# Transposed tiles copied out of PSUM by VectorE while the first pass leads by over 30 steps, with new per-stretch constants

## Chip, cores and metric

One core of one Trainium2 chip runs the whole kernel in one launch. The metric is the device time of that launch in microseconds (us). Engines: TensorE (PE, with PEld for its weight loads), VectorE (DVE), ScalarE (ACT), GpSimd (POOL), and SyncE (SP), which issues the DMAs.

## What is computed

Two layers over 2048 tokens of 512 channels, 32 heads of 16 channels, an FFN of 1792. Both layers use the same weights.

```python
def _A_ref(x, wqkv, wo):                       # attention, Dh = 16
    qkv = (x @ wqkv).reshape(B, S, 3, H, Dh).transpose(2, 0, 3, 1, 4)
    q, k, v = qkv[0], qkv[1], qkv[2]
    scores = jnp.einsum("bhqd,bhkd->bhqk", q, k) * (Dh ** -0.5)
    p = _softmax(scores, axis=-1)
    o = jnp.einsum("bhqk,bhkd->bhqd", p, v)
    return o.transpose(0, 2, 1, 3).reshape(B, S, D) @ wo
def _B_ref(x, w_gate, w_up, w_down):
    return (_gelu(x @ w_gate) * (x @ w_up)) @ w_down
x = x + _A_ref(_layernorm(x), A_wqkv, A_wo)    # layer 0
x = x + _B_ref(_layernorm(x), B_w_gate, B_w_up, B_w_down)
x = x + _A_ref(_layernorm(x), A_wqkv, A_wo)    # layer 1
x = x + _B_ref(_layernorm(x), B_w_gate, B_w_up, B_w_down)
```

## The kernel before

**Units and the two passes.** Four heads make a group (eight groups). Queries are cut into blocks: four of 512 tokens in layer 0, and 512, 512, 512, 256, 256 in layer 1. A unit is one block of queries and one group of heads. Every unit goes through two passes over the scores.

- The *first pass* finds each query's maximum. `p1_emit` makes score tiles with queries on the partitions and 512 keys in a PSUM bank (matmuls of L1648), and VectorE takes the maximum of one or two such tiles in one instruction (L1663) into `PM`. The maximum is written back into spare rows of `QT`, through `MT` and small DMAs on SP's queue, so that the second pass subtracts it inside its matmul.
- The *second pass* (`p2_emit`, `p2_tile`) makes the scores again with keys on the partitions (L1518), ScalarE takes the exponential of one or two banks (L1494) into slots of `SCR` (called `PT` in the code), and `pv_emit` multiplies them with the values into PSUM bank 7 (L1542); a column of ones gives the sums.
- A *fold* moves first-pass work from VectorE to ScalarE. POOL makes the difference of two key blocks (`KD`, L1279), PE makes its scores (L1467), ScalarE takes the Relu of one or two such tiles into `PT` slots (L1474), and one custom VectorE instruction (L1658) adds this to the other block's tile and takes the maximum of the sum, so that one instruction covers two tiles. The pair is then worth two tiles in the count of steps.

**Steps and the lead.** `pos["p1"]` and `pos["p2"]` count work in pairs of 512-wide tiles; each pass has 2048 steps. The lead is `pos["p1"] - pos["p2"]`. The second pass of a unit can start only when the first pass of that unit is done, so the lead can't fall below about one unit (32 steps for 512 queries).

**The order.** All instructions are put into the queues by a planner that runs when the kernel is built. It keeps a clock for each engine and for each tile, and at each turn chooses what PE gets next: first-pass matmuls, second-pass matmuls, a fold, a value product, a piece of a projection or FFN product ("chains", with due times counted in first-pass steps), or a filler matmul (`warm_emit`, L1687). Within an engine the order is that of the planner; between engines there are semaphores. The planner's constants are read every 16 first-pass steps from a row of `PLAN` (129 rows of 21 values), in this order:

```python
SPC, SPLIT, S1C, S2C, OV, LIM, NT, P2B, LAG, LAGT, FL, GL, FX, AHD, DUE, DUEM, PIECE, GP, NPV, PB, OVF = PLAN[stretch[0]]
```

S1C and S2C say how long before VectorE or ScalarE runs dry the next score matmuls are put in; LIM, OV and OVF, by how much a chain may hold these up. Above a lead of LAG the second pass gets more PSUM banks and the first pass is held to single ones. `want_fold` folds while the lead is below n/16 + FL, with n the queries of the block (40 for 512 and FL = 8); while a gelu stage is on, below GL; and in the last 360 first-pass steps (from step 1688) below `GLE` = 20. PIECE and GP are the numbers of matmuls in one piece of a chain.

**Copies out of PSUM.** `transpose_tile` (L816) transposes a 128-token tile by four PE transposes into one PSUM bank (bank 3, at times others) and has it copied to SBUF by `evac`, with `fast=True`: to `XNT` (normalized input of the projections and of the FFN) or to `ATTT` (attention output, ahead of the output projection). `proj` (to `SG`) and `vproj` (to `VP`) call `evac` without `fast`. `evac` puts the copy on VectorE (L686) or ScalarE (L688) as `pick` says:

```python
def pick(dve_ok=True):
    if not can_p1[0] and can_p2[0]:
        return "dve"
    if can_p1[0] and not can_p2[0]:
        return "act"
    if not can_p1[0] and not can_p2[0]:
        return "dve" if clk["dve"] <= clk["act"] else "act"
    return "dve" if pos["p1"] - pos["p2"] > LAGT else "act"
```

`can_p1` and `can_p2` say whether a first-pass or second-pass step can be put in now. With both, the copy goes to VectorE only above a lead of LAGT (84 in most rows). `pick` also places the residual sums (`x_add`) and the products of the up projection (L1234, L1240).

**Stages.** In the profile, block ends in layer 0 lie near 363, 664, 965 and 1267 us (output projection, then layernorm and FFN of that block), in layer 1 near 1599, 1897, 2183, 2350 and 2491 us. The FFN's gelu stage (L1221) stops the second pass while it lasts.

Of the kernel before, what the change touches and what calls it, by code (L numbers as in the profile page):

```python
# [310 lines left out]
def _build(nc, x_in, wqkv, wo, wg, wu, wd, out, layer_blocks=((512, 512, 512, 512), (512, 512, 512, 256, 256)),  # L311
# [16 lines left out]
    with es:  # L328
# [355 lines left out]
        def evac(dst, src, r, w, n, fast=False):  # L684
            if pick() == "dve":
                emit("dve", lambda e: e.tensor_copy(dst, src), r=r, w=w, dur=0.065 + n / (1900.0 if fast else 963.0))  # L686
            else:
                emit("act", lambda e: e.activation(dst, src, ACTF.Copy), r=r, w=w, dur=0.055 + n / 1200.0)  # L688
# [1241 lines left out]
```

## Time and profile before

| | us |
|---|---|
| median of 3 runs (2524.16 to 2528.22) | 2525.06 |
| the profiled execution's own time | 2523.95 |
| span of that profile, first to last instruction | 2522.2 |
| copies to XNT and ATTT on ScalarE (L688), 91 | 37.0 + 19.9 busy |
| copies to XNT and ATTT on VectorE (L686), 5 | 1.7 for the four to XNT |
| DVE idle, 60 to 2400 us | 48 |
| ACT idle, 60 to 2400 us | 128 |

How to read the profile's page: "busy" is the time in which an engine worked; the slices give it in tenths over forty equal parts of the span. The chain of waits goes back from the last instruction, at each step to whatever released it. A group's line reads: line of the kernel, engine, operation, output <- input with shapes, count | busy us, mean ns of one | idle time just before, and what ended it. "issue" is time for which the profile shows no cause. Neighbouring instructions of one engine overlap in their listed durations, so the distance from start to start is the time that one more of them takes.

```profile
PE   8999999999999999999999999999999999999999
DVE  7999999999999999999998999999999999999973
ACT  7799999999999999999979899999999999989996
PEclk9999999999999999999999999999999999999999
```

The granted PE clock is full in every slice, and only the first and the last slices of VectorE and ScalarE are visibly empty.

### The profile page before, as it was taken

To read this page: it belongs to the slowest core of one execution; us is meant where nothing else is said; L and a number is where in the kernel's file an instruction comes from. 1 tells how busy PE (TensorE), PEld (TensorE's weight loads), DVE (VectorE), ACT (ScalarE), POOL (GpSimd) and SP (SyncE) were. 2 spreads that over 40 slices of the span, in tenths; PEclk is the share of its full clock that TensorE was granted. 3 is DMA by queue.
4 is the path that set the end of the run, shared out by engine and by line. 5 is a ranking of instruction groups with operands and counts; after the bars stand their busy time and mean duration, and the time that the engine had idled before them with its cause. 6 is when DMAs were issued, how large, how long until landed. Compare 5 with 4: busy or idle time off the path is not lost.

```text
span 2522.2 us, 68091 instructions
## 1 busy us (share of the span) xinstructions
PE 2409.2 (96%) x29682; PEld 1161.1 (46%) x29881; DVE 2403.7 (95%) x3131; ACT 2353.2 (93%) x3267; POOL 683.9 (27%) x1119
## 2 busy tenths in 40 slices
PE   8999999999999999999999999999999999999999
PEld 3444443445434444344434455434453445534556
DVE  7999999999999999999998999999999999999973
ACT  7799999999999999999979899999999999989996
POOL 4111223321332213431133311341113311442300
PEclk9999999999999999999999999999999999999999
DMA  3110000000000000000000000000000000000000
GB/s 102 38 56 6 4 9 2 4 2 2 8 1 4 2 4 6 3 3 14 13 3 4 17 2 2 8 4 10 2 4 6 6 6 3 4 3 14 2 7 6
DMA packets 27419, 25.07 MB, mean 10 GB/s; under 512 B 9456, under 2 KB 26096, under 8 KB 27120
## 3 DMA queue, kind: packets, MB, share of 16 engines
q1 hardware_dynamic: 27120, 20.71, 2.9%
q8 instruction: 234, 3.83, 0.7%
q14 instruction: 65, 0.53, 0.1%
HBM read 9.70 MB, written 2.10 MB: 5 GB/s over the span
## 4 chain that ended last, share of the span: by engine, by line
PE 42%; DVE 32%; ACT 24%; issue 1%; POOL 0%; ACTq 0%
DVE PM L1663 30%; ACT SCR L1494 22%; PE PS L1648 14%; PE PS L671 12%; PE PS L1542 9%; PE PS L1687 4%; PE PS L1518 3%; ACT SCR L1474 1%; DVE SCR L1658 1%; PE PS L816 1%; ACT AO L1114 0%; PE PS L1467 0%; ACT XNT L688 0%; ACT ATTT L688 0%; ACT SG L688 0%
## 5 line engine op out<-in xcount | busy, mean ns | idle before, releaser
L1663 DVE TENSOR_REDUCE PM<-PS 128x1 f32<-128x512 f32 (+1 forms) x2513 | 2216.6, 944 | 52.0 <-PE PS L1518 24.1
L1494 ACT ACTIVATE SCR<-PS 128x1024 bf16<-128x1024 f32 (+1 forms) x2533 | 2008.2, 899 | 59.2 <-PE PS L1518 43.4
L1648 PE MATMUL PS<-KT,QT 32*128 32x512 bf16 x3923 | 1013.1, 384 | 49.4 <-DVE PM L1663 31.9
L1518 PE MATMUL PS<-QT,KT 32*128 32x512 bf16 (+1 forms) x4608 | 924.0, 360 | 7.5 <-ACT SCR L1494 6.3
L1542 PE MATMUL PS<-VP,SCR 128*128 128x51 bf16 (+1 forms) x16384 | 800.8, 187 | 12.3 <-ACT SCR L1494 8.0
L1542 PEld LDWEIGHTS PS<-VP,SCR 128*128 128x128 bf16 x16384 | 568.3, 96 | 486.8 <-issue 424.8
L1648 PEld LDWEIGHTS PS<-KT,QT 32*128 32x128 bf16 x3923 | 242.2, 91 | 547.8 <-DVE PM L1663 324.5
L1687 PE MATMUL PS<-WV,ZER 128*128 128x240 bf16 x2425 | 425.2, 266 | 4.7 <-ACT SCR L1494 4.5
L1096 POOL TENSOR_TENSOR RL<-ACCS,CM 128x16 f32<-128x16 f32 (+1 forms) x63 | 174.5, 2769 | 564.5 <-ACT ACCS L1086 564.3
L1518 PEld LDWEIGHTS PS<-QT,KT 32*128 32x128 bf16 x4608 | 230.2, 91 | 69.3 <-ACT SCR L1494 42.5
L1687 PEld LDWEIGHTS PS<-WV,ZER 128*128 128x128 bf16 x2425 | 185.1, 96 | 63.9 <-issue 48.5
L1242 POOL TENSOR_TENSOR HT<-HT,AO 128x512 bf16<-128x512 bf16 (+1 forms) x107 | 119.5, 1119 | 236.9 <-ACT AO L1240 236.9
L996 POOL TENSOR_TENSOR PM<-PM 128x16 f32<-128x16 f32 (+2 forms) x130 | 30.2, 232 | 379.1 <-DVE PM L1663 373.9
L1279 POOL TENSOR_TENSOR KD<-KT 128x512 bf16<-128x512 bf16 x72 | 82.9, 1152 | 173.9 <-PE PS L1467 166.0
L671 PE MATMUL PS<-XNT,WU 128*128 128x512 bf16 (+1 forms) x447 | 116.3, 353 | 7.3 <-issue 6.2
L671 PE MATMUL PS<-WD,HT 128*128 128x512 bf16 x381 | 115.5, 380 | 7.2 <-issue 5.4
L671 PE MATMUL PS<-XNT,WG 128*128 128x512 bf16 (+1 forms) x488 | 116.3, 357 | 3.6 <-ACT HT L1221 2.1
L1116 POOL TENSOR_TENSOR X<-X,AO 128x512 f32<-128x512 f32 x46 | 58.3, 1266 | 218.8 <-ACT AO L1114 218.8
L1658 DVE CUSTOM_DVE_ANT_0 SCR<-PS,SCR 128x512 bf16<-128x512 f32 x173 | 111.7, 685 | 3.1 <-PE PS L1467 0.6
L1474 ACT ACTIVATE SCR<-PS 128x512 bf16<-128x512 f32 (+1 forms) x121 | 97.1, 802 | 18.7 <-PE PS L1467 18.3
L1221 ACT ACTIVATE HT<-PS 128x512 bf16<-128x512 f32 (+1 forms) x126 | 69.3, 550 | 36.2 <-PE PS L671 33.4
L671 PEld LDWEIGHTS PS<-XNT,WG 128*128 128x128 bf16 x504 | 39.2, 97 | 55.0 <-issue 29.6
(111 smaller groups left out, 991.0 us busy)
## 6 DMA issues: line engine op xcount, KB each, us to landing
KT<-SG SPq DMA_DIRECT2D x64, 64.0 KB
QT<-MT SPq DMA_DIRECT2D x236, 1.0 KB
QT<-SG SPq DMA_DIRECT2D x56, 64.0 KB
out_dram<-AO SPq DMA_DIRECT2D x16, 128.0 KB, 1.7
WG<-in_B_w_gate_dram SPq DMA_DIRECT2D x4, 448.0 KB, 4.8
WU<-in_B_w_up_dram SPq DMA_DIRECT2D x4, 448.0 KB, 4.7
WD<-in_B_w_down_dram SPq DMA_DIRECT2D x4, 384.0 KB, 4.7
QT<-MT SPq DMA_DIRECT2D x68, 0.5 KB
```

Source lines behind the costliest of these rows:

```text
L671: ins = e.matmul(out_ap, lhsT=l, rhs=r_, start=(i == 0), stop=(i == n - 1))
L1096: emit("pool", lambda e: e.tensor_tensor(RL[:, s, 0:4 * nq], lsum, CM1[:, 0:4 * nq], op=ALU.pow), r=[("ACCS", s), ("CM1",)], w=[("RL", s)] ...
L1242: emit("pool", lambda e, ft=ft, o=o: e.tensor_tensor(HT[:, ft, 0:n], HT[:, ft, 0:n], AO[:, o, 0:n], op=ALU.mult), r=[("AO", o), ("HT", ft) ...
L1279: emit("pool", lambda e: e.tensor_tensor(KD[:, s, :], KT[:, g, ka * 512:(ka + 1) * 512], KT[:, g, kb * 512:(kb + 1) * 512], op=ALU.subtrac ...
L1474: emit("act", lambda e: e.activation(PT[:, s0:s0 + cnt, :], PS[:, bk:bk + cnt, :], ACTF.Relu), r=bks, w=[("PT", s0 + d) for d in range(cnt ...
L1494: emit("act", lambda e: e.activation(dst, src, ACTF.Exp, scale=DH ** -0.5), r=[BK[bk + i] for i in range(cnt)], w=[("PT", i) for i in slot ...
L1518: ins = e.matmul(bank(bk)[:, i * n:(i + 1) * n], lhsT=KT[32 * j:32 * j + 32, g, kt * 128:(kt + 1) * 128], rhs=QT[32 * j:32 * j + 32, s, 0: ...
L1542: ins = e.matmul(acc, lhsT=PT[:, slot, i * n + qt * 128:i * n + (qt + 1) * 128], rhs=AP(VP, (kt * H + 4 * g + j) * 17, [[NTT * H * 17, 128 ...
L1648: ins = e.matmul(bank(b), lhsT=QT[32 * j:32 * j + 32, s, qt * 128:(qt + 1) * 128], rhs=KT[32 * j:32 * j + 32, g, kb * 512:(kb + 1) * 512], ...
L1658: emit("dve", lambda e, i=i, b=b, sl=sl: e.tensor_tensor_reduce(PT[:, sl, :], bank(b), PT[:, sl, :], 1.0, -3.0e38, ALU.add, ALU.max, po[:, ...
L1663: emit("dve", lambda e: e.tensor_reduce(po, PS[:, bs[0]:bs[0] + cnt, :], axis=AX.X, op=ALU.max), r=bks, w=[("PM", sm) + h[1:] for h in hs] ...
L1687: return e.matmul(PS[:, b, NACC:512], lhsT=ZER[:, :], rhs=WV[:, 0, 0:512 - NACC], start=(b != 7), stop=(b != 7), skip_group_check=True)
```

## The change

`evac` puts a copy with `fast` (the transposed tiles alone) on VectorE when the lead is above TRL = 30 and at least one of the two passes can go on; where that does not hold, `pick` decides as before. TRD = 0 asks only that the first pass has begun.

```diff
-           ... HNA=3, TNA=3, PB=1, OVF=0.0, ...
+           ... HNA=3, TNA=3, TRD=0, TRL=30, PB=1, OVF=0.0, ...
@@
         def evac(dst, src, r, w, n, fast=False):
-            if pick() == "dve":
+            if fast and pos["p1"] > TRD and pos["p1"] - pos["p2"] > TRL and (can_p1[0] or can_p2[0]) or pick() == "dve":
                 emit("dve", lambda e: e.tensor_copy(dst, src), r=r, w=w, dur=0.065 + n / (1900.0 if fast else 963.0))
```

95 of the 129 rows of PLAN are replaced (row r holds from first-pass step 16 r on). DUE changes in 43 of them, LAG in 41, GL in 40, S2C in 34, S1C in 31, PIECE in 26, FL in 25, LAGT in 11. Some of them:

```diff
@@ rows 4, 6 (steps 64, 96) @@
-    (0.2, 0.1, 0.55, 0.42, 0.3, -0.05, 1, 0, 22, 84, 8, 20, 0.3, 2.0, 0, 6, 1, 2, 9, 1, 0.0),
+    (0.2, 0.1, 0.55, 0.22, 0.3, -0.05, 1, 0, 22, 84, 8, 20, 0.3, 2.0, 0, 6, 4, 2, 9, 1, 0.0),
-    (0.2, 0.1, 0.55, 0.42, 0.3, -0.05, 1, 0, 22, 84, 8, 20, 0.3, 2.0, 0, 6, 1, 2, 9, 1, 0.0),
+    (0.2, 0.1, 0.55, 0.62, 0.3, -0.05, 1, 2, 22, 84, 8, 20, 0.3, 2.0, 0, 6, 2, 2, 9, 1, 0.0),
...
@@ rows 33, 50 (steps 528, 800) @@
-    (0.2, 0.25, 0.45, 0.42, 0.3, 0.05, 2, 1, 126, 84, 3, 60, 0.3, 2.0, -20, 2, 1, 2, 7, 1, 0.2),
+    (0.2, 0.25, 0.45, 0.42, 0.2, 0.05, 2, 1, 126, 84, -7, 60, 0.3, 2.0, -20, -14, 1, 2, 7, 1, 0.2),
-    (0.3, 0.2, 0.45, 0.42, 0.3, -0.05, 1, 1, 62, 84, 8, 40, 0.5, 1.5, 0, 2, 2, 2, 7, 3, 0.0),
+    (0.15, 0.2, 0.45, 0.32, 0.5, -0.05, 1, 1, 70, 84, -2, 80, -0.1, 2.0, 10, -14, 2, 1, 9, 1, 0.0),
...
@@ rows 67, 68 (steps 1072, 1088) @@
-    (0.1, 0.35, 0.15, 0.52, 0.3, -0.15, 1, 1, 70, 84, 8, 20, -0.3, 1.5, 0, 2, 2, 4, 7, 1, 0.0),
-    (0.1, 0.25, 0.45, 0.32, 0.3, -0.05, 1, 1, 70, 84, 13, 60, -0.1, 2.0, 0, 2, 1, 4, 5, 1, 0.0),
+    (0.1, 0.35, 0.0, 0.52, 0.3, -0.15, 1, 1, 86, 84, 8, 20, -0.3, 1.5, 0, 2, 2, 4, 7, 1, 0.0),
+    (0.1, 0.35, 0.0, 0.62, 0.3, -0.15, 1, 1, 86, 84, 8, 20, -0.3, 1.5, 0, 2, 1, 4, 7, 1, 0.0),
...
@@ rows 117, 120 (steps 1872, 1920) @@
-    (0.15, 0.15, 0.65, 0.02, 0.1, -0.05, 3, 0, 38, 84, 53, 80, 0.3, 2.5, -10, 2, 2, 2, 3, 4, 0.1),
+    (0.15, 0.15, 0.65, 0.02, 0.1, -0.05, 3, 0, 62, 84, 33, 80, 0.3, 4.0, 10, 2, 1, 2, 3, 1, 0.0),
-    (0.4, 0.15, 0.65, 0.42, 0.3, -0.05, 3, 0, 5, 84, 8, 60, 0.3, 3.5, -5, 6, 2, 3, 3, 1, -0.05),
+    (0.15, 0.15, 0.65, 0.02, 0.1, -0.05, 3, 0, 62, 84, 33, 80, 0.3, 6.0, 5, 2, 1, 2, 3, 1, 0.0),
```

More of the change, by code (lines that the diff above doesn't have):

```diff
@@ L311, in _build @@
 def _build(nc, x_in, wqkv, wo, wg, wu, wd, out, layer_blocks=((512, 512, 512, 512), (512, 512, 512, 256, 256)),
-           n_ahead=6, n_pre=6, S1C=0.45, S2C=0.42, OV=0.3, PD=80, FDUE=20, LIM=-0.05, NT=1, AHD=2.0, DUEM=2, FDL2=0, OPD=12, URG=0.3, ft_tok=512, n_pt=8, n_qt=8, SPLIT=0.15, SPC=0.1, PVC=47, WARM=0.55, WARML=0.42, NPV=7, BOOST=0.0, LAG=62, LAGT=84, GP=2, SING=0, DUE=0, END=360, LAGE=10, FD=205, FDL=-10, QD=32, KD_=16, VD=20, FL=8, FMAX=6, NKD=2, FLOOK=2, FX=0.3, GF=1, NSPL=3, HSPL=0, TSPL=1, HNA=3, TNA=3, PB=1, OVF=0.0, LNP=0, FNP=1, NSG=3, LNT=12, HV=16, TW=0.95, HF=60, VS=14, SO=1.0, SF=1, SP=0, FAST=1, TG=0, GS=2, P2B=1, PIECE=2, GL=60, GLE=20, HARD=-1e9):
+           n_ahead=6, n_pre=6, S1C=0.45, S2C=0.42, OV=0.3, PD=80, FDUE=20, LIM=-0.05, NT=1, AHD=2.0, DUEM=2, FDL2=0, OPD=12, URG=0.3, ft_tok=512, n_pt=8, n_qt=8, SPLIT=0.15, SPC=0.1, PVC=47, WARM=0.55, WARML=0.42, NPV=7, BOOST=0.0, LAG=62, LAGT=84, GP=2, SING=0, DUE=0, END=360, LAGE=10, FD=205, FDL=-10, QD=32, KD_=16, VD=20, FL=8, FMAX=6, NKD=2, FLOOK=2, FX=0.3, GF=1, NSPL=3, HSPL=0, TSPL=1, HNA=3, TNA=3, TRD=0, TRL=30, PB=1, OVF=0.0, LNP=0, FNP=1, NSG=3, LNT=12, HV=16, TW=0.95, HF=60, VS=14, SO=1.0, SF=1, SP=0, FAST=1, TG=0, GS=2, P2B=1, PIECE=2, GL=60, GLE=20, HARD=-1e9):
     S = x_in.shape[1]
```

162 rows, old and new, of the table PLAN are left out of this document.

## The prediction

> **What bounds the kernel now.** I read the page's head and busy shares first, then the chain of waits, then the groups of instructions by form, then busy time by stage, and last the order of time around single copies.
>
> ```profile
> span 2522.2 us, 68091 instructions
> PE 2409.2 (96%) x29682; PEld 1161.1 (46%) x29881; DVE 2403.7 (95%) x3131; ACT 2353.2 (93%) x3267; POOL 683.9 (27%) x1119
> PE 42%; DVE 32%; ACT 24%; issue 1%; POOL 0%; ACTq 0%
> DVE PM L1663 30%; ACT SCR L1494 22%; PE PS L1648 14%; PE PS L671 12%; PE PS L1542 9%; PE PS L1687 4%; PE PS L1518 3%; ACT SCR L1474 1%; DVE SCR L1658 1%; PE PS L816 1%; ACT AO L1114 0%; PE PS L1467 0%; ACT XNT L688 0%; ACT ATTT L688 0%; ACT SG L688 0%
> ```
>
> Three engines are nearly full. PE's share is the weakest bound of the three: L1687 (425.2 us by form) is filler that the planner puts into gaps. What can't be dropped is VectorE's maximum over the scores (L1663, first pass) and ScalarE's exponential (L1494, second pass): 2216.6 and 2008.2 us. The transposed copies themselves have 0% of the chain, so nothing is gained at their own place; they count as engine time. By stage (busy us: PE, PEld, DVE, ACT, POOL):
>
> ```profile
> 60.00:360.00 300.00, 285.94 (x3677) 143.57 (x3681) 295.62 (x418) 280.10 (x320) 51.08 (x105) 1.00 0.08 23
> 700.00:940.00 240.00, 228.97 (x2915) 109.06 (x2934) 236.16 (x310) 231.57 (x304) 65.73 (x88) 1.00 0.01 3
> 1260.00:1300.00 40.00, 38.23 (x245) 14.10 (x248) 36.50 (x56) 28.53 (x44) 14.58 (x25) 1.00 0.02 5
> 1300.00:1590.00 290.00, 281.34 (x3482) 135.21 (x3500) 276.26 (x351) 268.21 (x344) 72.58 (x98) 1.00 0.02 6
> 2400.00:2522.00 122.00, 115.91 (x1556) 69.70 (x1558) 68.73 (x109) 95.36 (x143) 6.56 (x13) 1.00 0.02 7
> ```
>
> DVE is at 98.5% in the first two rows and idles 3.5 and 13.7 us in the two stages around the change of layer. Over the fifteen such stages that make up 60 to 2400 DVE idles 48 us and ACT 128 (length less busy, added). From 2400 on the first pass runs out (its last reduce starts at 2469.5) and ACT's second pass ends the chain. So DVE is the tighter engine up to 2400, ACT behind it, and neither alone sets the end.
>
> **The change, part one: who copies.** Which tiles move follows from the lead of the first pass at each copy. I counted it in the trace: a 1024-wide reduce is one step, a 512-wide half a step, a custom one (L1658) one step with its folded partner; likewise the exponentials. Both counts end at 2048. At the 91 copies that ACT now makes,
>
> ```profile
> L688 ACT ACTIVATE XNT<-PS 128x512 bf16<-128x512 bf16 x60 | 37.0, 624 | 10.2 <-PE PS L816 9.8
> L688 ACT ACTIVATE ATTT<-PS 128x512 bf16<-128x512 bf16 x31 | 19.9, 643 | 2.2 <-PE PS L816 2.1
> L686 DVE COPY XNT<-PS 128x512 bf16<-128x512 bf16 x4 | 1.7, 419 | 2.4 <-PE PS L816 2.4
> ```
>
> the lead is 0 to 21 for 13 in the head, 0 for three in the tail, 29.5 for two near 2210 us, and 30.5 to 78.5 for the other 73. So 73 move (63 up to 1923 us, ten behind). The floor of the lead is about 40 because the planner folds when it falls below n/16 + FL = 32 + 8; a threshold of 30 lies under it. New rows with FL at -2 or -7 lie at some clusters, but there the lead would still have to fall by ten steps first, and the eight copies of a cluster cost DVE only 2.3 steps; I take 70 to 75.
>
> The profile's durations overlap for neighbours, so the price is the distance from a start to the next start:
>
> ```profile
> 31.50 2.06 ACT L688 ACTIVATE XNT<-PS 128x512 bf16<-128x512 bf16 x4
> 33.40 0.67 ACT L791 ACTIVATE X<-HT 128x512 f32<-128x512 bf16 x1
> 952.15 0.41 DVE L686 COPY XNT<-PS 128x512 bf16<-128x512 bf16 x1
> 952.48 1.21 DVE L1663 TENSOR_REDUCE PM<-PS 128x2 f32<-128x1024 f32 x1
> 953.62 0.69 DVE L763 BATCH_NORM_STATS2 ST<-X 128x6 f32<-128x512 f32 x1
> ```
>
> ACT: (33.40 - 31.50)/4 = 0.475 us a copy, DVE: 952.48 - 952.15 = 0.33. Removed from ACT: 73 x 0.475 = 34.7 us. Added to DVE: 73 x 0.33 = 24.1. Nothing else is issued by a copy: no DMA, no POOL or SP instruction. The wait is the same (for the four transposes of L816) but now DVE's: behind it in that queue stand the next reduces, and for those wait the first-pass matmuls that need their banks (324.5 us of weight-load idle is already put down to L1663). If a copy reaches DVE before PE is done, the loss is of the size that DVE copies show now: 3.2 us over five (2.4 XNT, 0.8 ATTT), 0.64 each, all of it in head and tail. The one DVE copy between 360 and 2400 (952.15) started within its queue's run of work and waited for nothing, so I price this wait at 0, with one such wait for each of ten clusters, 6.4 us, as the other end.
>
> What the time makes of 34.7 off and 24.1 on has three values. If DVE alone binds and nothing is given back: **+24.1**. If ACT alone binds: **-34.7**. Between them lies the exchange that the kernel already has: a folded pair replaces two 1024-wide reduces (2 x 1.14 = 2.28 us, 953.62 - 952.48 each) by two custom ones, and costs one 1024-wide Relu on ACT:
>
> ```profile
> 1277.23 0.69 DVE L1658 CUSTOM_DVE_ANT_0 SCR<-PS,SCR 128x512 bf16<-128x512 f32 x1
> 1277.84 0.69 DVE L1658 CUSTOM_DVE_ANT_0 SCR<-PS,SCR 128x512 bf16<-128x512 f32 x1
> 1278.45 0.69 DVE L1658 CUSTOM_DVE_ANT_0 SCR<-PS,SCR 128x512 bf16<-128x512 f32 x1
> 1267.47 1.03 ACT L1474 ACTIVATE SCR<-PS 128x1024 bf16<-128x1024 f32 x1
> 1268.38 0.62 ACT L688 ACTIVATE ATTT<-PS 128x512 bf16<-128x512 bf16 x1
> ```
>
> 2.28 - 2 x 0.61 = 1.06 us saved on DVE for 0.91 on ACT. For the 63 early copies, DVE +20.8 and ACT -29.9 are level after 50.7/1.97 = 26 pairs: DVE 20.8 - 27.3 = **-6.5**, ACT -29.9 + 23.4 = -6.5. Folds (173 custom instructions now) do occur up to 1942.7 us, and the rule makes them exactly when the lead falls. Behind step 1688 (about 2010 us) the code folds only below a lead of 20; there the ten late copies are worth between +3.3 (DVE) and -4.8 (ACT, which ends the chain); I take 0. Part one: **-6.5**.
>
> The Trainium skill, page "Perfetto Trace Analysis", section "Optimizing Scalar/DVE Operations", speaks against the move: an operation that DVE does quicker may still belong on Scalar when DVE is saturated. The trace agrees with both halves (0.33 against 0.475 us; DVE at 98.5%), and by that rule the value to take would be DVE's +24.1.
>
> **Part two: the constants.** 95 of 129 rows differ. They issue nothing and take nothing away; they move the moment at which instructions are put into the queues (S1C, S2C, LIM), who gets banks (LAG, P2B), when folds are made (FL, GL) and how projections are cut (PIECE, GP). None of this shows as an operation, so it is bounded by idle time. From above: a new order can lose what the worst stage loses now; 1300 to 1590 idles 13.7 us on DVE in 290, 4.7%, against 1.5% in 700 to 940; if a quarter of the span got that way, 2340/4 x 3.2% = +19. From below: if the stages from 1260 to 1590 came down to 1.5% idle, DVE would win 17.2 - 5.0 = 12 us, and from ACT's 19.9 idle us in 60 to 360 some 3 more through folds: -15. The rows at steps 1056 to 1103 (1260 to 1310 us), where the idle time lies, are changed, and those of 1600 to 1700 hardly. Between the ends I take **-3**, nearer to none than to either, since the idle of the saturated stages (1.5%) is what most rows can act on.
>
> **Sum.** -6.5 - 3 = -9.5 against the profiled execution (span 2522.2, run 2523.95), which lies 1.1 below the median of the runs shown, 2525.06. Forecast **2515.5 us**, own range 2508 to 2520.
>
> **Rivals.** (1) *The stages around the change of layer close up*: part two reaches its -15, with part one -6.5: 2503.5. For it: 17.2 us of DVE idle in 330, mostly behind second-pass matmuls (L1518, 11.6 us between 1260 and 1600). Against: it falls where the lead stands at 50 to 80 because the second pass stands for the gelu stage, and the change leaves that stage as it is. (2) *Covered*: the lead falls from 40 to 33, no fold is made in exchange, and the next gelu stage, where the lead rises to 70 or 80 anyway, makes the copies free on both sides: 2525, between 2520 and 2530. For it: after each cluster the lead grows by 20 to 40 steps. Against: DVE has no idle time in which to hide 24 us except 48 in all, spread over 2340. (3) *DVE becomes the bound at the block ends*: at 363, 635, 949, 1599 and 1897 us the lead stands at its floor, each copy delays the reduces behind it, PT slots or the gelu stage keep folds from being made, and ScalarE's second pass, one unit behind, stands for the same time. Price 24.1 less what the last ten and the 16 copies around the layer change (leads of 47 and more) don't cost, 26 x 0.33 = 8.6: +15.5, 2540.5. It decides once fewer than 12 of the 26 pairs are folded (20.8 - 12 x 1.06 - 3 = +5). For it: DVE 98% busy; against: folds are triggered by this very lead.
>
> **How the numbers follow.** A measurement of this kernel can tell about 0.2% (5 us) from no change, so faster means below 2520.0 and slower above 2530.1. Forecast 0.42, rival 1 0.20, rival 2 0.17, rival 3 0.21. Faster: 0.42 + 0.20, less 0.01 for the forecast's upper edge: 0.61; same 0.18; slower 0.21. The predicted time is the forecast's. The range takes in rival 1 with 5 us beyond it, rival 2, and the near edge of rival 3: 2498 to 2532.
>
> **What would show it.** Line L686 should have some 78 XNT and ATTT copies on DVE at about 0.41 us, L688 some 18 on ACT. L1658 should rise from 173 by some 50; busy time of DVE and ACT should both fall by about 6 to 7 us. If L1658 stays and DVE's busy time grows by 20 or more, rival 3 holds; if the lead after the clusters is lower and the span the same, rival 2; if idle time of DVE between 1260 and 1590 halves, rival 1. Wrong would be, above all, copies that wait on DVE for L816 by more than a microsecond a cluster, or a span that changes through stages in which no copy was moved.

## The result, and the profile after

Ten runs of each: 2532.05 us (2531.44 to 2534.34) with the change against 2524.86 (2524.16 to 2528.22) before, a ratio of 1.0028, 95% interval 1.0020 to 1.0036. The kernel became 7 us slower; forecast were 2515.5 us and a gain.

The head of the page after, its chain by engine, and the groups that answer to those of before:

```profile
span 2530.2 us, 68181 instructions
PE 2421.0 (96%) x29691; PEld 1165.8 (46%) x29897; DVE 2416.6 (96%) x3202; ACT 2343.3 (93%) x3252; POOL 683.8 (27%) x1126
PE 44%; DVE 36%; ACT 19%; issue 1%; POOL 0%; ACTq 0%
L1663 DVE TENSOR_REDUCE PM<-PS 128x2 f32<-128x1024 f32 (+1 forms) x2473 | 2196.5, 950 | 47.6 <-PE PS L1518 24.7
L1494 ACT ACTIVATE SCR<-PS 128x1024 bf16<-128x1024 f32 (+1 forms) x2583 | 2014.5, 875 | 72.7 <-PE PS L1518 51.9
L1658 DVE CUSTOM_DVE_ANT_0 SCR<-PS,SCR 128x512 bf16<-128x512 f32 x191 | 123.3, 686 | 4.5 <-PE PS L1648 1.6
L1474 ACT ACTIVATE SCR<-PS 128x512 bf16<-128x512 f32 (+1 forms) x131 | 106.1, 810 | 21.0 <-PE PS L1467 20.6
```

The copies, in the views of the tiles XNT and ATTT (shortest, median and longest ns; first and last start):

```profile
L686 DVE COPY XNT<-PS x46: 377/415/425, 10.3 to 2374.9; 128x512 bf16<-128x512 bf16 x46
L688 ACT ACTIVATE XNT<-PS x18: 591/597/641, 19.5 to 2508.2; 128x512 bf16<-128x512 bf16 x18
L686 DVE COPY ATTT<-PS x31: 382/414/425, 362.5 to 2499.8; 128x512 bf16<-128x512 bf16 x31
L688 ACT ACTIVATE ATTT<-PS x1: 597/597/597, 2499.6 to 2499.6; 128x512 bf16<-128x512 bf16 x1
```

So 77 copies are on VectorE where 5 were: 72 moved (73 by the new rule, and `pick` sends one fewer). L1658 rose from 173 to 191: nine more folded pairs. VectorE is busy 12.9 us longer (2416.6 against 2403.7) and idle 4.9 us less (span less busy: 113.6 against 118.5); the difference is the 8.0 us of the span. ScalarE is busy 9.9 us less and waits more, 51.9 us instead of 43.4 for second-pass matmuls. On this balance alone the case looks like rival 3, VectorE as the bound. The stages shown before, after the change (the last one now ends at 2530):

```profile
60.00:360.00 300.00, 288.86 (x3675) 143.46 (x3678) 294.95 (x430) 282.14 (x319) 52.40 (x108) 1.00 0.08 23
700.00:940.00 240.00, 232.21 (x2909) 110.96 (x2928) 236.21 (x306) 231.90 (x321) 65.86 (x88) 1.00 0.01 3
1260.00:1300.00 40.00, 38.85 (x295) 15.76 (x297) 37.62 (x63) 29.21 (x41) 14.62 (x25) 1.00 0.04 9
1300.00:1590.00 290.00, 279.15 (x3456) 134.42 (x3473) 274.67 (x342) 265.67 (x345) 72.82 (x98) 1.00 0.03 6
2400.00:2530.00 130.00, 123.28 (x1671) 73.14 (x1672) 78.44 (x121) 103.78 (x163) 8.90 (x17) 1.00 0.02 6
```

Of the five busy times in a row VectorE's is the third (294.95 in the first row, 295.62 before). It hardly moves in the first four rows; no stage stands out. The last row takes in the delay (VectorE 78.44 against 68.73 before). Where the time came in shows when the two passes are compared step by step. How many us later than in the kernel before each pass of the changed kernel reaches a step (counted as in the prediction, on a straight line between two counts):

| step | 272 | 528 | 784 | 1040 | 1296 | 1552 | 1808 | last |
|---|---|---|---|---|---|---|---|---|
| first pass | -0.3 | -0.2 | 2.1 | 4.0 | 9.4 | 6.6 | 7.4 | 8.7 |
| second pass | -1.4 | -0.3 | -0.4 | 2.5 | 1.4 | 4.5 | 5.4 | 8.0 |

The second pass passes step 784, at 976 us, 0.4 us early, with 28 moved copies behind it. It loses 6 us between its steps 1360 and 1424 (1.7 to 7.7 late), at 1709 to 1782 us, a stretch without one moved copy. The first pass, whose maxima are VectorE's work, falls behind sooner: 4.0 us late at 1040 and 9.4 at 1296, at 1233 and 1562 us, with twelve moved copies between. So the table by itself neither convicts the copies nor clears them.

### The profile page after: what moved, and what is told of

It reads as the page before. It is cut to its first block, busy times and chain, and to the rows that moved or that the text cites. A ratio compares the mean times of both kernels' runs of the same rounds, so it can differ in the third digit from the quotient of the medians.

```text
span 2530.2 us, 68181 instructions
## 1 busy us (share of the span) xinstructions
PE 2421.0 (96%) x29691; PEld 1165.8 (46%) x29897; DVE 2416.6 (96%) x3202; ACT 2343.3 (93%) x3252; POOL 683.8 (27%) x1126
## 4 chain that ended last, share of the span: by engine, by line
PE 44%; DVE 36%; ACT 19%; issue 1%; POOL 0%; ACTq 0%
DVE PM L1663 34%; ACT SCR L1494 18%; PE PS L1648 14%; PE PS L671 12%; PE PS L1542 9%; PE PS L1518 4%; PE PS L1687 4%; DVE SCR L1658 1%; PE PS L816 1%; ACT SCR L1474 1%; PE PS L1467 1%; ACT AO L1240 0%; ACT AO L1114 0%; ACT SG L688 0%; DVE MT L1000 0%
## 5 line engine op out<-in xcount | busy, mean ns | idle before, releaser
L1663 DVE TENSOR_REDUCE PM<-PS 128x2 f32<-128x1024 f32 (+1 forms) x2473 | 2196.5, 950 | 47.6 <-PE PS L1518 24.7
L1494 ACT ACTIVATE SCR<-PS 128x1024 bf16<-128x1024 f32 (+1 forms) x2583 | 2014.5, 875 | 72.7 <-PE PS L1518 51.9
L1518 PE MATMUL PS<-QT,KT 32*128 32x512 bf16 (+1 forms) x4608 | 940.3, 360 | 8.8 <-ACT SCR L1494 6.7
L1687 PE MATMUL PS<-WV,ZER 128*128 128x240 bf16 x2441 | 430.4, 266 | 3.7 <-ACT SCR L1494 3.5
L1658 DVE CUSTOM_DVE_ANT_0 SCR<-PS,SCR 128x512 bf16<-128x512 f32 x191 | 123.3, 686 | 4.5 <-PE PS L1648 1.6
L1474 ACT ACTIVATE SCR<-PS 128x512 bf16<-128x512 f32 (+1 forms) x131 | 106.1, 810 | 21.0 <-PE PS L1467 20.6
```

What stands on the lines that cost most here:

```text
L1474: emit("act", lambda e: e.activation(PT[:, s0:s0 + cnt, :], PS[:, bk:bk + cnt, :], ACTF.Relu), r=bks, w=[("PT", s0 + d) for d in range(cnt ...
L1494: emit("act", lambda e: e.activation(dst, src, ACTF.Exp, scale=DH ** -0.5), r=[BK[bk + i] for i in range(cnt)], w=[("PT", i) for i in slot ...
L1518: ins = e.matmul(bank(bk)[:, i * n:(i + 1) * n], lhsT=KT[32 * j:32 * j + 32, g, kt * 128:(kt + 1) * 128], rhs=QT[32 * j:32 * j + 32, s, 0: ...
L1658: emit("dve", lambda e, i=i, b=b, sl=sl: e.tensor_tensor_reduce(PT[:, sl, :], bank(b), PT[:, sl, :], 1.0, -3.0e38, ALU.add, ALU.max, po[:, ...
L1663: emit("dve", lambda e: e.tensor_reduce(po, PS[:, bs[0]:bs[0] + cnt, :], axis=AX.X, op=ALU.max), r=bks, w=[("PM", sm) + h[1:] for h in hs] ...
L1687: return e.matmul(PS[:, b, NACC:512], lhsT=ZER[:, :], rhs=WV[:, 0, 0:512 - NACC], start=(b != 7), stop=(b != 7), skip_group_check=True)
```

## The experiments

The theories at the start: A, the copies are what costs, because VectorE sets the pace; B, they are harmless and the new constants cost; C, ScalarE sets the pace. Since a new rule or new rows make the planner lay out another order from the first fork on, each was tried in two ways: planned anew, and with the queues of a kernel kept as they are and the copies alone put elsewhere.

**Copies moved by hand, both ways.** `emit` gets an argument that names the engine whose queue receives the instruction; the planner's clocks go on as if it had not been moved, so PE's and POOL's queues stay the same.

```diff
-        def emit(eng, fn, r=(), w=(), dur=0.1, grp=None, nd=1):
-            sch.op(eng, fn, r=r, w=w, grp=grp, nd=nd)
+        def emit(eng, fn, r=(), w=(), dur=0.1, grp=None, nd=1, on=None):
+            sch.op(on or eng, fn, r=r, w=w, grp=grp, nd=nd)
@@ evac, in the kernel before @@
+            elif fast and pos["p1"] - pos["p2"] > 30 and (can_p1[0] or can_p2[0]):
+                emit("act", lambda e: e.tensor_copy(dst, src), r=r, w=w, dur=0.055 + n / 1200.0, on="dve")
@@ evac, in the changed kernel @@
+            if fast and pos["p1"] > TRD and pos["p1"] - pos["p2"] > TRL and (can_p1[0] or can_p2[0]) and pick() != "dve":
+                emit("dve", lambda e: e.activation(dst, src, ACTF.Copy), r=r, w=w, dur=0.065 + n / 1900.0, on="act")
```

> The kernel before with its queues as they are (all of PE's and POOL's instructions in the same order, the same 173 custom instructions), but 73 transposed copies taken out of ScalarE's queue and put into VectorE's at the same point of the order. Theory A (VectorE sets the pace up to 2400 us, and nothing is folded in exchange): 73 x 0.33 = 24 us more work on VectorE, of which the idle time of the engine (48 us in 2340) takes a fifth: +15 to +24, 2540 to 2549. Theory B (the copies are harmless, the new constants are what costs): within 3 us of 2525. Theory C (ScalarE sets the pace): 73 x 0.475 = 35 us less work there, -5 or better.

> The changed kernel with its queues as they are (191 custom instructions, all of PE's in the same order), but the 73 transposed copies that the new rule sends to VectorE put into ScalarE's queue at the same point. Theory A: VectorE loses 24 us of work; its load is then below that of the kernel before (2416.6 - 24 = 2393 against 2404 us busy) while ScalarE's rises by 35 to 2378: 2515 to 2528, no slower than before. Theory B: stays at 2530 or above, since the constants remain.

Measured: 2539.49 us for the first, 1.0061 (1.0048 to 1.0073) of the kernel before, +15; 2553.53 for the second, 1.0114 (1.0100 to 1.0128) of the kernel before and 21 us above the changed one. The first agrees with theory A, and with neither B nor C. The second contradicts A: to take the same copies off VectorE made things worse still. B's "2530 or above" takes it in, but gives no reason for the 21 us. Each order is dear to change, in either direction. Part of both losses goes with a lower granted clock (last section), but not all: the one run of each whose clock was 1.000 took 2536.71 and 2550.09 us, still 12 and 18 us too long. In the first, the second pass is late by 1.2 us at step 272, 3.2 at 528, 5.4 at 784 and 9.9 at 1040: a little more with each block end, as 73 copies without a gap for them would do.

**Half changes, planned anew.** One kernel has the new `evac` with the PLAN of before, the other the PLAN of after with the old `evac`.

> The new rule for the copies with the constants of before, order planned anew: 75 copies moved, 170 custom instructions (3 fewer than before, so no exchange at all). Theory A: +15 to +25, 2540 to 2550. Theory B: 2522 to 2528. If an order that is planned anew under constants made for another one costs by itself, this adds to both.

> The new constants with the old rule for the copies, order planned anew: 90 copies on ScalarE, 171 custom instructions. Theory A with harmless constants: 2520 to 2528. Theory B: 2531 or above. Planned anew under constants made for another order, it may cost up to 10 us more in either.

Measured: 2559.28 us (1.0139, 1.0123 to 1.0154) and 2561.45 (1.0145, 1.0132 to 1.0159). Each half costs 35 to 37 us, both together 7; no theory had a cost of this size. Neither part can be priced alone. The second pass's loss grows nearly everywhere from step 784 on (e1_copies_alone: 4.0, 6.0, 19.3, 25.5, 31.6 us at 784, 1040, 1296, 1552, 1808; e2_constants_alone: 6.6, 19.0, 26.5, 26.8, 31.2). That suggested theory D: rows of constants fit one order.

**A nudge.** No rule and no row is changed, only one of the planner's estimates, by 0.0001 or 0.001 us.

```diff
@@ p1_before_nudged and p4_after_nudged_2 @@
-                    t += 0.006
+                    t += 0.0061
@@ p2_after_nudged and p3_before_nudged_2 @@
-        SEM = 0.06
+        SEM = 0.061
```

> The kernel before with its constants and its rule for the copies; only one of the planner's estimates, the gap between row-tiled matmuls, is 0.0061 us instead of 0.006, so that the order forks. Theory D (the rows of constants fit one single order; any other order under them loses some 30 us, and the 2559 and 2561 of the two half changes are that loss): 2540 to 2565. Theory E (the loss of the half changes is the copies' or the constants' own): 2522 to 2528.

> The changed kernel with its constants and its rule; only the planner's estimate for a semaphore is 0.061 us instead of 0.06. Theory D: 2555 to 2580, as far above 2532 as the half changes were above 2525. Theory E: 2529 to 2535.

> The kernel before with the nudge that was put on the changed kernel (the semaphore estimate 0.061 instead of 0.06). Theory D: 2540 to 2565 once more.

> The changed kernel with the nudge that was put on the kernel before (0.0061 instead of 0.006). Theory D: 2550 to 2580. If the new rule costs something in any order, the two nudged kernels with it lie above the two without it by the same amount; if not, the four lie mixed.

Measured:

| | rows fit | nudged | nudged 2 |
|---|---|---|---|
| old rule, old rows | 2524.86 | 2550.63 (p1) | 2545.09 (p3) |
| new rule, new rows | 2532.05 | 2571.21 (p2) | 2557.32 (p4) |
| new rule, old rows | | 2559.28 (e1) | |
| old rule, new rows | | 2561.45 (e2) | |

Ratios to the kernel before: 1.0105 (1.0090 to 1.0121) for p1, 1.0182 (1.0169 to 1.0196) for p2, 1.0081 (1.0065 to 1.0096) for p3, 1.0128 (1.0114 to 1.0142) for p4. Theory D's forecasts hold in all four: an order that forks under rows fitted to another costs 20 to 39 us against its own kernel, with the rule and the constants untouched. The 35 and 37 of the half changes are within that. The page of p1_before_nudged shows little that a reader could have priced:

```profile
span 2549.4 us, 68186 instructions
PE 2434.8 (96%) x29715; PEld 1165.7 (46%) x29922; DVE 2417.6 (95%) x3148; ACT 2357.0 (92%) x3287; POOL 682.2 (27%) x1109
```

Every engine is as full as before within one point of its share, over a span longer by 27 us. A part does show when the forks are counted: the four nudged orders have 10 to 16 custom instructions fewer than their own kernels (p1 161 against 173), so fewer folds, which at the prediction's 1.06 us a pair is 5 to 8.5 us of VectorE's time; and VectorE is busy 12 to 25 us longer (13.9 in p1). A fork changes the amount of work as well as its order. For comparison the retuned kernel of the last experiments, 32 us shorter:

```profile
span 2517.2 us, 68280 instructions
PE 2431.7 (97%) x29881; PEld 1159.3 (46%) x29881; DVE 2400.9 (95%) x3127; ACT 2351.9 (93%) x3254; POOL 686.0 (27%) x1122
```

Its VectorE and ScalarE are busy for about as long as in the kernel before (2400.9 and 2351.9 us against 2403.7 and 2353.2). Of the 5 us between these two spans VectorE is busy 2.8 less and idle 2.3 less: they have no single place.

**Copies left out.** To learn what the copies weigh in each order, `emit` skips them (`skip=True` where `on=` stood above); ATTT is set to zero once at the start.

> Leaves out the 73 transposed copies that the new rule would move (their PE transposes stay; PE goes on with what XNT and ATTT hold); all other queues of the kernel before are unchanged, so ScalarE has 35 us less work and nobody waits for a copy. If ScalarE's work set the pace: -15 to -35. Theory F (in a fixed order relief of one engine is worth little, because every queue waits for PE and PE's order was laid out around both): 0 to -6.

> Leaves out the same kind of 73 copies of the changed kernel, which are VectorE's there: 24 us less work on VectorE. If the copies on VectorE are what made it slower (theory A): 2532 down by 8 to 15, to 2517 to 2524. Theory F: 0 to -5 against the changed kernel's 2532.

Measured: 2522.89 (0.9992, 0.9983 to 1.0001) and 2532.63 (1.0031, 1.0020 to 1.0041, both against the kernel before). Busy time from 60 to 2400 us (PE, PEld, DVE, ACT, POOL) first of the kernel before and then of it without the copies:

```profile
60.00:2400.00 2340.00, 2244.74 (x27875) 1070.48 (x28064) 2291.83 (x2961) 2211.49 (x3037) 650.50 (x1050) 1.00 0.03 8
```

```profile
60.00:2400.00 2340.00, 2243.56 (x27894) 1069.71 (x28082) 2293.75 (x2965) 2186.83 (x2968) 651.33 (x1051) 1.00 0.03 8
```

And of the changed kernel, then of that without the copies:

```profile
60.00:2400.00 2340.00, 2249.24 (x27767) 1071.81 (x27962) 2295.02 (x3021) 2193.12 (x3001) 647.93 (x1053) 1.00 0.03 8
```

```profile
60.00:2400.00 2340.00, 2250.01 (x27767) 1071.93 (x27963) 2276.10 (x2949) 2193.08 (x3001) 646.49 (x1053) 1.00 0.03 8
```

In the first pair ScalarE loses 24.7 us of busy time and the other engines do what they did in the same time; in the second VectorE loses 18.9. (Both are less than the 34.7 and 24.1 priced, which are distances from start to start.) The time stays. Theory F's forecasts hold, and theory A has fallen for the changed kernel's order as it lies: there the copies on VectorE, at 98% busy, cost nothing (2532.05 with, 2532.63 without). It isn't shown what order the planner would have laid out had the copies cost VectorE nothing. In one table, the same 73 copies in the two fixed orders:

| queues of | no copies | on ScalarE | on VectorE |
|---|---|---|---|
| the kernel before | 2522.9 | 2524.9 (as planned) | 2539.5 |
| the changed kernel | 2532.6 | 2553.5 | 2532.05 (as planned) |

Where the planner put them they are worth 0 to 2 us; on the other engine 17 to 21 (14 and 17 in the runs with a clock of 1.000).

**Fewer fillers.** Does PE's own queue hold the pace, so that relief elsewhere can't show?

```diff
         def warm_emit(b):
+            n_warm[0] += 1
-            emit_pe(warm_fn(b), 1, 512 - NACC, r=[("ZER",), ("WV",)], w=[BK[b]])
+            emit_pe(warm_fn(b), 1, 512 - NACC, r=[("ZER",), ("WV",)], w=[BK[b]], skip=n_warm[0] % 8 == 0 and pos["p1"] > 32)
```

> The kernel before with every eighth filler matmul of L1687 behind step 32 left out (298 of 2425, some 0.1 us of PE each, 31 us), every other instruction in its place. Theory G (the pace of a fixed order is PE's own queue with its fillers, which is why relief of ScalarE or VectorE was worth nothing): -10 to -30 while the granted clock stays at 1. Theory H (no engine alone sets it; the queues are locked to each other at each step, and a gap that was filled is now a wait): 0 to -5. If the granted clock falls, slower.

> The same cut (300 of 2441 fillers) in the changed kernel. Theory G: 2532 down to 2502 to 2522. Theory H: 2527 to 2532, so that the 7 us to the kernel before remain.

Measured: 2520.66 (0.9983, 0.9974 to 0.9992) and 2528.44 (1.0014, 1.0005 to 1.0022): -4 us for each, some 31 us of PE's time gone (fillers lie 0.103 us apart from start to start, the median of the trace before). Theory G falls: PE's fillers are not the pace either. H's range fits; what it says, that some queue waits for another at each step and that work taken from one of them leaves a longer wait, is inferred from that. The 8 us between the two kernels remain.

**Retuned rows.** For both kernels rows were altered in steps, which were kept when the planner's own last clock came out earlier. Most of the altered rows differ in one to six values; some, eleven in the kernel before, differ in more than half of their 21. Two rows of r2_before_constants_again:

```diff
-    (0.2, 0.1, 0.55, 0.42, 0.3, -0.05, 1, 0, 22, 84, 8, 20, 0.3, 2.0, 0, 6, 1, 2, 9, 1, 0.0),
+    (0.2, 0.1, 0.55, 0.42, 0.3, -0.1, 1, 0, 22, 84, 8, 20, 0.3, 2.0, 0, 6, 1, 2, 9, 1, 0.0),
...
-    (0.2, 0.1, 0.55, 0.62, 0.3, -0.05, 1, 2, 14, 84, 8, 60, 0.3, 2.0, -5, 2, 4, 3, 9, 1, 0.05),
+    (0.2, 0, 0.55, 0.62, 0.3, -0.05, 1, 2, 14, 84, 8, 60, 0.3, 2.0, -5, 2, 2, 3, 9, 1, 0.05),
```

> The changed kernel with 56 of its 129 rows of constants altered again, by small steps that were kept where the planner's own last clock came out earlier; 77 copies on VectorE and 191 custom instructions as in the changed kernel. Theory D (the time is the fit of the rows to one order): faster than the changed kernel by a few us, 2525 to 2530. Theory A (the copies on VectorE are what costs): within 2 us of 2532.

> The same treatment of the kernel before (62 rows altered, 6 copies on VectorE): theory D: 2517 to 2522, so that the gap between the two rules stays as it was, 5 to 10 us; if the kernel before had been at the end of what rows can give, 2524 to 2526.

Measured: 2526.89 (1.0009, 1.0000 to 1.0018) and 2518.65 (0.9976, 0.9967 to 0.9986). Each gained 5 to 6 us with as many folds as before (191 and 173 custom instructions) and at most one copy moved (77 on VectorE in the first, as before; 6 in the second, 5 before), so this gain is the rows'. The gap between the rules stayed, 8 us. The retuned kernel before beats both kernels of this case, and with the fillers cut as well it does so by more:

> The kernel before with the retuned constants of r2_before_constants_again and every eighth filler behind step 32 left out. If the gains add: 2525 - 6 - 4 = 2515, range 2513 to 2518. If both take the same waits: 2518 to 2520.

Measured: 2515.74 us, 0.9966 (0.9952 to 0.9979). That is 8.2 us under the kernel before in the same series (2523.9), where the two gains, 5.8 and 4.1, would make 9.9 in full. Most of both adds up, though the interval just takes in the gain of the rows alone.

## Why the prediction was wrong

**What moved, and its price: right.** 72 copies against 73, 0.415 us listed on VectorE and 0.331 from start to start (median of the trace after), against the 0.33 priced. They wait for L816 in head and tail only (2.4 us for XNT and 0.8 for ATTT, the same as before), as priced.

**The exchange: the step that failed first.** "For the 63 early copies, DVE +20.8 and ACT -29.9 are level after 50.7/1.97 = 26 pairs" took folds for a valve that opens by itself. Nine pairs came. L1663 fell by 20.1 us and L1658 rose by 11.6, so VectorE got back 8.5 us and not 27.3. The lead did fall at the copies, but at most of them not below the threshold: at 19 of the 32 moved copies up to 990 us the row in force (FL = -2 or -7; at eleven of them lowered by the new rows) asks for a fold, outside a gelu stage, only below 30 or 25, and the lead there is never under 32.0 (at 989.8 us). Elsewhere it stayed near its threshold, as with 33.5 at 685.9 us under one of 35 (FL = 3). The prediction names such rows and still took all 26 pairs. And under the old rows, where e1_copies_alone moved 75 copies, there were 170 custom instructions, none more than before.

**Engine time as value: the step that was wrong in kind.** Behind the -6.5 and behind both ends, +24.1 and -34.7, stands the idea that a us taken from or given to a nearly full engine is worth some part of a us. The copies left out show that it is worth 0 to 2 us of 35 on ScalarE and nothing of 24 on VectorE, in an order laid out with them; the copies moved show 17 to 21 us on an engine whose queue has no place for them. 93 to 96% busy on three engines did not mean here that one of them has a price. With nine pairs in place of 26 the prediction's own sum comes to +8.3 (20.8 - 9 x 1.06 - 3), near the 7 measured; since the copies left out gained nothing, nothing shows that VectorE's time is the reason, and the nearness may be luck.

**The constants: mis-sized, and not a term of its own.** "They issue nothing and take nothing away" is true, and bounding them by idle time in the present order, -15 to +19 with -3 taken, was the mistake. A change that forks the order is a new draw, and four draws with nothing else changed lay 20 to 39 us above their fitted order. The new rule forks it too: under the old rows it lost 34 us (2559.3 - 2524.9), and the new rows won back 27 of them (2559.3 - 2532.05). The 7 us of the result are what they did not win back; that is a balance of runs and names no wait or queue that holds them.

**The rivals.** The sign was rival 3's, and its 2540.5 is near what the copies cost in the old order (2539.5, a loss that grows with each block end). The rule of the Trainium skill that was weighed there ("Perfetto Trace Analysis", "Optimizing Scalar/DVE Operations": with DVE saturated, work may be better placed on Scalar) agrees with that run, but not with the changed kernel, where VectorE is as full and the copies cost nothing. Rival 2, the copies covered, is what the changed kernel's own order shows. None of the rivals had the new order itself as its mechanism, though the diff says that 95 of 129 rows are replaced; only the upper bound of part two, +19, had room for a worse one.

**What stays open.** Whether the new rule costs something in every order. For it: 8 us of gap after the same treatment of the rows, and the nudged orders of the new pair (2571, 2557) above those of the old (2551, 2545), though by 7 us with the one nudge and by 26 with the other. VectorE is also busy longer under the new rule, by 12.9 us in the kernels of this case and by 13.7 in the retuned ones (2414.6 against 2400.9), since the folds pay for only a part of the copies; that the planner spreads its order over this extra work, so that it costs time which leaving the copies out afterwards can't bring back, is a rival that no run here tests. Against: the second pass of the changed kernel goes by 28 moved copies without loss, and of the two half changes the one with the new rule is the quicker. Two draws each can't decide it, and one treatment of the rows isn't the end of what they can give. So the runs show what the 7 us are not, the engine time of the copies in their order; which part of the new order holds them stays open.

## What to carry to other kernels

Where an order is laid out by a planner whose constants were fitted to it, measure the fork first: nudge an estimate by a thousandth of a us and run. Here that cost 0.8 to 1.5%, more than the change under study, and the balance of busy time before the change told neither its size nor its sign. To price an instruction in such a kernel, keep the queues and leave it out, or put it into the other queue by hand; if leaving it out gains nothing, moving it within the same order has nothing to win.

## What was not expected of the hardware

In two of the kernels with altered queues the granted clock of TensorE fell to half for a longer stretch. In the profile of s2_after_copies_back, 20 us behind 638 us ran at half clock, at a block end with twelve copies; VectorE and ScalarE both fell to 77 or 78% busy there (31.14 and 30.69 of 40 us), and 7.8 of the 24.4 us by which that execution is late come in between its steps 494 and 520 of the second pass:

```profile
630.00:670.00 40.00, 38.55 (x385) 18.09 (x382) 31.14 (x37) 30.69 (x43) 9.84 (x17) 0.74 0.05 12
```

The changed kernel, with the same instructions of PE and a full clock:

```profile
630.00:670.00 40.00, 37.80 (x475) 19.15 (x476) 39.38 (x53) 35.19 (x49) 11.43 (x20) 1.00 0.05 12
```

PE looks as busy in both (38.55 and 37.80) and gets through 385 matmuls instead of 475. So part of the 21 us of that experiment is the clock's, not the copies' alone: the run at 1.000 was 3.4 us below the median. What brought the clock down isn't shown. With an eighth of the fillers left out the profiled execution had 37.5 us at half clock behind 1419 us (0.69 in this window) and took 2534.24 us, where the median of the runs is 2520.66:

```profile
1400.00:1460.00 60.00, 57.74 (x497) 23.46 (x499) 47.61 (x61) 38.89 (x55) 20.81 (x29) 0.69 0.05 11
```

In the kernel before this happened once: without an eighth of the fillers most runs are 4 us shorter and this one of the twelve is 10 us longer, where none of the 21 runs with all fillers in that series took more than 2528.14. The changed kernel with the same cut stayed between 2526.9 and 2530.7 in eleven runs. So whether the fillers left out are the reason is not shown.
